# A two-dimensional Fourier mixing layer and a maxout network on one core: the sequence transform regrouped, with its intermediate sent through DRAM

## The chip, the core and the metric

The kernel runs on one core of one Trainium2 chip. The metric is the device time in microseconds of one execution. A core has five engines that run their own instruction streams in order: TensorE (PE, with weight loads shown as PEld), VectorE (DVE), ScalarE (ACT), GpSimd (POOL) and SyncE (SP), beside 16 DMA engines. SP and POOL issue most DMAs here.

## The reference

```python
X = np.fft.fft(x, axis=1)          # x: (8, 3072, 256), float32
X = np.fft.fft(X, axis=2)
x = X.real.reshape(24576, 256)
h = np.maximum(np.maximum(x @ w1, x @ w2), x @ w3)   # each w: (256, 768)
out = h @ w_out                                      # w_out: (768, 256), float32 result
```

There are eight batches of 3072 tokens with 256 features.

## The kernel before

Everything is bf16 with float32 accumulation. The feature transform (256 points) is folded into the weights at the start (`product`, `prep_first`, `prep_second`: tables `gE`, `gO`, `gD`, `gw`). What is left per batch is the sequence transform (3072 points), and then the network. The real part of a transform of real data has a symmetry, so only the frequencies 0 to 1535 are transformed (`NHALF`), as an even part `tE` and an odd part `tO`, each 128 x 1536; a token and its mirror come from sums and differences of the two.

**The main loop.** For each batch b there are three blocks of 512 tokens, and in each block six units (one for each 128 columns of the hidden layer), 18 units a batch (`UNITS`). A unit issues four matmuls of 128x512 for the token itself (`unit_plus`, L415 and L416), the activation and maximum of them (`unit_out`: L429 on ACT, L430 on DVE), two more 128x512 matmuls for the mirrored token of the unit before (`unit_minus`, L423), and then ten steps of the second layer of the block before (`l2_some(10)`: matmuls L439, L455 and L463, the sum on DVE at L468, and the stores). A 128-token result leaves by two stores: the tokens themselves by SP (L483) and the mirrored tokens, which stand in falling order, by an indirect DMA of POOL (L473).

**The transform of the next batch** is cut into pieces that a hand-written plan (`at(batch, unit, fn)`) puts at the ends of units, behind `l2_some(10)`. 3072 is handled as 24 times 128:

- `load_chunk` loads a quarter of the next x in float32 by four SP DMAs (L100) of 24 partitions each, in runs of 64 values (256 bytes). `turn_chunk` casts and reorders it on POOL (L118, four casts a batch).
- `s0` to `s12` (L337): 64 small matmuls a batch, with a 96x128 piece of x as the stationary operand and the constant `m24blk` (96x96) moving; ACT casts each group of five out of PSUM into `ub` (L339).
- `fA0` to `fC1` (`fold`, L350 to L373): DVE adds and subtracts mirrored halves of `ub` into `zE` and `zO`.
- `kE0` to `kO2` and `end` (L387 to L406): the second stage, six groups of 128-wide matmuls with `zE` and `zO` as stationary operand against the tables `cos_t`, `sin_t`, `nsin_t`; ACT casts each group into `tE` or `tO` (L399).

For batches from the third on, the pieces start at unit 5 of the batch before and end at unit 17. Batch 0 does all of this ahead of the main loop, after the tables have been made and after a few warm-up matmuls (L565).

Of the kernel before, what the change touches and what calls it, by code (L numbers as in the profile page):

```python
# [19 lines left out]
def _reduce(nc, w, v, q, period, rnd, neg):  # L20

    shape = list(v.shape)
    for c in (rnd, neg):
        assert c.shape[0] == shape[0]
    wide = [shape[0], v.free_size()]
    nc.vector.scalar_tensor_tensor(out=q, in0=v, scalar=1.0 / period,
                                   in1=rnd.to_broadcast(wide), op0=ALU.mult, op1=ALU.add)
    nc.vector.scalar_tensor_tensor(out=q, in0=q, scalar=-ROUND,
                                   in1=neg.to_broadcast(wide), op0=ALU.add, op1=ALU.mult)
    nc.vector.tensor_tensor(out=w, in0=v, in1=q, op=ALU.add)  # L30


@with_exitstack
def kernel(
# [18 lines left out]

    DLS = ((20, 25), (25, 30), (30, 35), (35, 40), (40, 45),
           (15, 20), (45, 50), (10, 15), (50, 55),
           (5, 10), (55, 60), (60, 64), (0, 5))
# [7 lines left out]
    xs_pool = ctx.enter_context(tc.tile_pool(name="xs", bufs=4))  # L64
    x0_pool = ctx.enter_context(tc.tile_pool(name="x0", bufs=2))
    u_pool = ctx.enter_context(tc.tile_pool(name="ubuf", bufs=1))
    z_pool = ctx.enter_context(tc.tile_pool(name="zbuf", bufs=1))
    t_pool = ctx.enter_context(tc.tile_pool(name="tbuf", bufs=2))

    m24blk = consts.tile([96, 96], BF16, tag="m24blk")  # L70
# [4 lines left out]
    cos_t = consts.tile([128, 13 * 128], BF16, tag="cos_t")  # L75
    sin_t = consts.tile([128, 13 * 128], BF16, tag="sin_t")
    nsin_t = consts.tile([128, 13 * 128], BF16, tag="nsin_t")
# [14 lines left out]
    zO = consts.tile([128, 26 * 128], BF16, tag="zO")  # L92

    def x_rows(b):
        return x[b].rearrange("(a bb) (g dl) -> g a bb dl", bb=128, g=4)

    def load_rows(eng, dst, b, r0, r1, after=None):
        xr = x_rows(b)
        for g in range(4):
            ld = eng.dma_start(out=dst[g * 24:(g + 1) * 24], in_=xr[g, :, r0:r1, :])  # L100
            if after is not None:
                tc.add_manual_dep(ld.ins, after.ins.name, AFTER, reason="weights first")

    def load_chunk(b, ch, after=None):
        xs = xs_pool.tile([96, 32 * 64], FP32, name="xs", tag="xs")
        load_rows(nc.sync, xs.rearrange("p (bb dl) -> p bb dl", dl=64), b,
                  ch * 32, ch * 32 + 32, after)
        return xs

    raw = {}  # L110
    turned = {}

    def turn_chunk(b, ch, after=None):

        if ch == 0:
            x0 = x0_pool.tile([96, 64 * 128], BF16, name="x0", tag="x0")
            turned[b] = x0.rearrange("p (dl bb) -> p dl bb", bb=128)
        cast = nc.gpsimd.tensor_copy(turned[b][:, :, ch * 32:(ch + 1) * 32],  # L118
                                     raw.pop((b, ch)).rearrange("p (bb dl) -> p dl bb", dl=64))
        if after is not None:  # L120
            tc.add_manual_dep(cast.ins, after.ins.name, AFTER, reason="folds first")
# [10 lines left out]
    HEAD = 80  # L132
    staged = []
    for (r0, eng) in ((80, nc.sync), (96, nc.scalar), (112, nc.sync)):
        xs = xs_pool.tile([96, 32 * 64], FP32, name="xs", tag="xs")
        load_rows(eng, xs[:, 0:16 * 64].rearrange("p (bb dl) -> p bb dl", dl=64), 0, r0, r0 + 16)
        staged.append((r0, xs))
# [3 lines left out]
    jm24 = gen.tile([96, 24], FP32, tag="jm24")  # L141
    iota(jm24[:, 0:13], [[1, 13]])
    iota(jm24[:, 13:24], [[-1, 11]], base=-1)
    g24 = gen.tile([96, 5], FP32, tag="g24")
    iota(g24, [[24, 5]])
    i13 = gen.tile([128, 13], FP32, tag="i13")
    iota(i13, [[1, 13]])
    j128 = gen.tile([128, 128], FP32, tag="j128")
    iota(j128, [[24, 128]])
    dvec = gen.tile([128, 128], FP32, tag="dvec")  # L150
    iota(dvec[:, 0:120], [[5, 12], [64, 2], [1, 5]])
    iota(dvec[:, 120:128], [[64, 2], [1, 4]], base=60)

    x0_first = x0_pool.tile([96, 128 * 64], BF16, name="x0", tag="x0")
    x0v = x0_first.rearrange("p (bb dl) -> p bb dl", dl=64)
    for (r0, r1) in ((0, 32), (32, 64), (64, 80)):
        load_rows(nc.gpsimd, x0v[:, r0:r1, :], 0, r0, r1)

    first_half = None
    for jh in range(2):  # L160
        for wsrc, wdst in ((moe_w1, w1_bf), (moe_w2, w2_bf), (moe_w3, w3_bf)):
            wld = nc.gpsimd.dma_start(
                out=wdst.rearrange("p (fc j) -> p fc j", fc=2)[:, :, jh * 384:(jh + 1) * 384],
                in_=wsrc.rearrange("(fc p) j -> p fc j", fc=2)[:, :, jh * 384:(jh + 1) * 384])
            if jh == 0 and wdst is w2_bf:
                first_half = wld
    nc.gpsimd.dma_start(out=wout_bf.rearrange("p (jc c) -> p jc c", jc=NJC),
                        in_=moe_w_out.rearrange("(jc p) c -> p jc c", jc=NJC))
    rows_f = gen.tile([128, 12 * B], FP32, tag="rows_f")
    rows_v = rows_f.rearrange("p (b r) -> p b r", r=12)  # L170
    iota(rows_v, [[S, B], [-1, 12]], base=S - 1, cm=-24)
    iota(rows_v[:, :, 11], [[S, B]], base=S - 24, cm=-24)
    late = gen.tile([128, 1], FP32, tag="late")
    nc.gpsimd.tensor_scalar(out=late, in0=pidx, scalar1=63.0, scalar2=float(S // 2 - 12),
                            op0=ALU.is_ge, op1=ALU.mult)
    nc.gpsimd.tensor_scalar(out=rows_v[:, :, 11], in0=rows_v[:, :, 11], scalar1=late,
                            scalar2=None, op0=ALU.add)
    nc.gpsimd.tensor_copy(rows_m, rows_f)
    zOr = zO.rearrange("p (r c) -> p r c", c=128)
    nc.gpsimd.memset(zO[:, 24 * 128:26 * 128], 0.0)  # L180
    nc.gpsimd.memset(zOr[:, 0:24, 0], 0.0)

    consts_of = {}
    for (name, value) in (("half_pi", 0.5 * math.pi), ("rnd", ROUND), ("n24", -24.0),
                          ("n256", -256.0), ("n3072", -3072.0)):
        c = gen.tile([128, 1], FP32, name=name, tag=name)
        nc.vector.memset(c, value)
        consts_of[name] = c
    s24 = gen.tile([96, 24], FP32, tag="s24")
    nc.vector.memset(s24[:, 0:13], 6.0)  # L190
    nc.vector.memset(s24[:, 13:24], 0.0)
# [4 lines left out]
    v24 = gen.tile([96, 24], FP32, tag="v24")  # L196
    q24 = gen.tile([96, 24], FP32, tag="q24")
    nc.vector.scalar_tensor_tensor(out=v24, in0=jm24, scalar=pidx[0:96], in1=s24,
                                   op0=ALU.mult, op1=ALU.add)
    _reduce(nc, v24, v24, q24, 24.0, consts_of["rnd"][0:96], consts_of["n24"][0:96])  # L200
    t24 = gen.tile([96, 24], FP32, tag="t24")
    nc.scalar.activation(out=t24, in_=v24, func=AX.Sin, scale=float(2.0 * math.pi / 24.0))
    ge24 = gen.tile([96, 5], FP32, tag="ge24")
    nc.vector.tensor_scalar(out=ge24, in0=g24, scalar1=pidx[0:96], scalar2=None,
                            op0=ALU.is_le)
    ind24 = gen.tile([96, 4], FP32, tag="ind24")
    nc.vector.tensor_tensor(out=ind24, in0=ge24[:, 0:4], in1=ge24[:, 1:5], op=ALU.subtract)
    pi13 = gen.tile([128, 13], FP32, tag="pi13")
    nc.vector.tensor_scalar(out=pi13, in0=i13, scalar1=pidx, scalar2=None, op0=ALU.mult)
    nc.vector.tensor_tensor(  # L210
        out=m24blk.rearrange("p (r g) -> p g r", g=4),
        in0=t24.unsqueeze(1).to_broadcast([96, 4, 24]),
        in1=ind24.unsqueeze(2).to_broadcast([96, 4, 24]), op=ALU.mult)

    w = gen.tile([128, 13 * 128], FP32, tag="w")
    v = gen.tile([128, 13 * 128], FP32, tag="v")
    q = gen.tile([128, 13 * 128], FP32, tag="q")
    turn = float(2.0 * math.pi / 3072.0)
    for (r0, r1) in ((0, 7), (7, 13)):
        cs = slice(r0 * 128, r1 * 128)  # L220
        n = r1 - r0
        nc.vector.scalar_tensor_tensor(
            out=v[:, cs].rearrange("p (r j) -> p r j", j=128),
            in0=j128.unsqueeze(1).to_broadcast([128, n, 128]), scalar=pidx,
            in1=pi13[:, r0:r1].unsqueeze(2).to_broadcast([128, n, 128]),
            op0=ALU.mult, op1=ALU.add)
        _reduce(nc, w[:, cs], v[:, cs], q[:, cs], 3072.0, consts_of["rnd"], consts_of["n3072"])
        nc.scalar.activation(out=sin_t[:, cs], in_=w[:, cs], func=AX.Sin, scale=turn)
# [503 lines left out]
```

## Time and profile before

| what | value |
|---|---|
| median of 3 runs | 432.07 us (430.92 to 433.14) |
| profiled execution: span from first to last instruction | 431.8 us |
| mean granted TensorE clock | 0.996 |
| busy: PE, DVE, ACT, POOL | 94%, 71%, 63%, 55% of the span |
| first unit of the main loop | starts at 33.2 us |
| DMA moved | 51.58 MB in 127333 packets, 109233 of them under 512 bytes |

The runs' times stand 0.3 us above the profiled span. The busy share of PE is a modelled one: matmuls overlap, so the pace of a group is read from the starts of its instructions, not from their durations.

### The profile page before, as it was taken

How to read it: one execution, taken by the hardware profiler on the slowest of the kernel's cores; microseconds unless marked ns; L12 is line 12 of the kernel's file. 1: busy time of each engine (PE TensorE's matmuls, PEld its weight loads, DVE VectorE, ACT ScalarE, POOL GpSimd, SP SyncE). 2: the span in 40 equal slices, each digit the busy share in tenths (PEclk: the TensorE clock that was granted, in tenths of full speed). 3: DMA queues.
4: the chain of work that ended last, by engine and by line, in shares of the span. 5: the costliest groups of instructions: out<-in, count | busy, mean ns of one | idle time of the engine just before them, and what ended most of it. 6: DMA issues, size and time to landing. Idle time of an engine off the chain costs nothing.

```text
span 431.8 us, 9121 instructions
## 1 busy us (share of the span) xinstructions
PE 404.8 (94%) x3196; PEld 271.1 (63%) x3252; DVE 307.7 (71%) x611; ACT 272.8 (63%) x512; POOL 238.0 (55%) x256
## 2 busy tenths in 40 slices
PE   0499979999999999999999999999999999999996
PEld 0175656666666666666666666667666666666665
DVE  7766748856886769576876679576876679667673
ACT  3576557666866676657765676757765676754650
POOL 7546762598249823984279624984369623214320
PEclk9989999999999999999999999999999999999999
DMA  9999999559731969159761969158762222111213
GB/s 115 111 160 124 128 139 192 152 113 174 147 107 53 179 131 204 63 99 160 145 145 73 167 127 199 73 97 155 148 141 74 74 63 74 62 56 52 105 66 130
DMA packets 127333, 51.58 MB, mean 119 GB/s; under 512 B 109233, under 2 KB 124344, under 8 KB 127288
## 3 DMA queue, kind: packets, MB, share of 16 engines
q1 hardware_dynamic: 104936, 35.80, 44.8%
q0 software_dynamic: 20624, 14.68, 17.8%
q10 hardware_dynamic: 1728, 0.52, 0.8%
q8 instruction: 25, 0.41, 0.4%
q14 instruction: 20, 0.16, 0.2%
HBM read 28.31 MB, written 25.17 MB: 124 GB/s over the span
## 4 chain that ended last, share of the span: by engine, by line
PE 84%; DVE 5%; ACT 4%; issue 2%; DMA 2%; POOL 1%; SPq 1%; ACTq 0%; DVEq 0%; POOLq 0%
PE po L439 27%; PE pse L415 14%; PE pse L423 13%; PE pse L416 11%; PE ps L337 6%; PE po L463 4%; PE pl L455 2%; DMA xs<-in_x_dram 2%; DVE hm L430 1%; ACT stmp L429 1%; PE warm L565 1%; PE psg L268 1%; PE ps L394 1%; DVE ot L468 1%; POOL x L118 1%
## 5 line engine op out<-in xcount | busy, mean ns | idle before, releaser
L429 ACT ACTIVATE stmp<-pse 128x512 bf16<-128x512 f32 x288 | 167.6, 605 | 57.4 <-PE pse L416 45.5
L473 POOL DMA_INDIRECT out_dram<-ot,rows_m x92 | 101.8, 1107 | 160.5 <-DVE ot L468 144.0
L430 DVE TENSOR_TENSOR hp<-pse,stmp 128x512 bf16<-128x512 f32 x144 | 99.3, 689 | 98.9 <-ACT stmp L429 64.9
L118 POOL CAST x<-xs 96x2048 bf16<-96x2048 f32 x28 | 104.6, 3745 | 11.3 <-DMA xs<-in_x_dram 8.8
L415 PE MATMUL pse<-tE,gE 128*128 128x512 bf16 x280 | 106.1, 379 | 2.2
L430 DVE TENSOR_TENSOR hm<-pse,stmp 128x512 bf16<-128x512 f32 x144 | 98.6, 685 | 6.3 <-ACT stmp L429 6.0
L416 PE MATMUL pse<-tO,gO 128*128 128x512 bf16 x245 | 92.7, 379 | 0.5
L439 PE MATMUL po<-wout_bf,hp 128*128 128x256 bf16 x576 | 86.1, 273 | 0.1
L423 PE MATMUL pse<-tO,gD 128*128 128x512 bf16 x284 | 84.9, 379 | 0.6
L439 PE MATMUL po<-wout_bf,hm 128*128 128x256 bf16 x576 | 78.6, 273 | 0.0
L339 ACT CAST ub<-ps 128x480 bf16<-128x480 f32 (+1 forms) x102 | 51.7, 556 | 37.2 <-PE ps L337 37.2
L439 PEld LDWEIGHTS <-hp 128*128 128x128 bf16 x576 | 56.4, 98 | 26.1
L439 PEld LDWEIGHTS <-hm 128*128 128x128 bf16 x576 | 56.4, 98 | 16.3
L468 DVE TENSOR_TENSOR ot<-po,even 128x512 f32<-128x512 f32 x92 | 62.7, 682 | 0.0
L423 PEld LDWEIGHTS <-gD 128*128 128x128 bf16 x288 | 27.7, 98 | 32.5 <-POOL gD L281 0.5
L416 PEld LDWEIGHTS <-gO 128*128 128x128 bf16 x288 | 28.1, 98 | 19.8 <-issue 1.6
L415 PEld LDWEIGHTS <-gE 128*128 128x128 bf16 x288 | 28.0, 97 | 19.5 <-issue 0.8
L337 PE MATMUL ps<-m24blk,x 96*128 96x96 bf16 x512 | 33.3, 213 | 2.7 <-POOL x L118 1.7
L463 PE MATMUL po<-gw,tO 128*128 128x512 bf16 x91 | 34.5, 379 | 0.0
L337 PEld LDWEIGHTS <-x 96*128 96x128 bf16 x512 | 30.5, 111 | 5.0 <-POOL x L118 2.0
L399 ACT CAST tO<-ps 128x512 bf16<-128x512 f32 x24 | 14.1, 586 | 22.4 <-PE ps L396 14.0
L459 ACT COPY even<-pl 128x512 f32<-128x512 f32 x46 | 27.3, 593 | 0.1
(127 smaller groups left out, 309.1 us busy)
## 6 DMA issues: line engine op xcount, KB each, us to landing
xs<-in_x_dram SPq DMA_DIRECT2D x112, 192.0 KB
out_dram<-ot SPq DMA_DIRECT2D x90, 128.0 KB
out_dram<-ot,rows_m POOLq DMA_INDIRECT x92, 4.4
w_bf<-in_moe_w_dram POOLq DMA_DIRECT2D x6, 192.0 KB, 5.6
out_dram<-ot SPq DMA_DIRECT2D x17, 64.0 KB
xs<-in_x_dram SPq DMA_DIRECT2D x8, 96.0 KB
x<-in_x_dram POOLq DMA_DIRECT2D x8, 96.0 KB, 11.5
xs<-in_x_dram ACTq DMA_DIRECT2D x4, 96.0 KB
```

What stands on the lines that cost most here:

```text
L118: cast = nc.gpsimd.tensor_copy(turned[b][:, :, ch * 32:(ch + 1) * 32], raw.pop((b, ch)).rearrange("p (bb dl) -> p dl bb", dl=64))
L337: nc.tensor.matmul(ps1[:, i * 96:(i + 1) * 96], x0[:, d0 + i, :], m24blk, start=True, stop=True)
L339: evict(out=self.ub[:, d0 * 96:d1 * 96].rearrange("p (c i) -> p c i", i=n), in_=ps1[:, 0:n * 96].rearrange("p (i c) -> p c i", c=96))
L415: nc.tensor.matmul(pse[:, 0:n], gE[i][:, js], te, start=True, stop=False)
L416: nc.tensor.matmul(pse[:, 0:n], gO[i][:, js], to, start=False, stop=True)
L423: nc.tensor.matmul(pse, gD[i][:, js], to, start=False, stop=True, skip_group_check=True)
L429: nc.scalar.activation(out=stmp[:, 0:n], in_=pses[0][:, 0:n], func=AX.Relu)
L430: nc.vector.tensor_tensor(out=dst, in0=src3, in1=stmp[:, 0:n], op=ALU.max)
L439: nc.tensor.matmul(po, hcols(jc), wout_bf[:, jc * 256:(jc + 1) * 256], start=False, stop=(jc == NJC - 1), skip_group_check=True)
L463: nc.tensor.matmul(po, to[:, cp], gw[:, 256:768], start=True, stop=True)
L468: nc.vector.tensor_tensor(out=ot.rearrange("p (h c) -> p h c", h=2), in0=po.rearrange("p (h c) -> p h c", h=2), in1=lin.unsqueeze(1).to_br ...
L473: stored(nc.gpsimd.indirect_dma_start(out, bass.IndirectOffsetOnAxis(ap=rows_m[0:128 - lo, b * 12 + slot: b * 12 + slot + 1], axis=0), ot[ ...
```

## The change

The sequence transform is regrouped as 96 runs of 32 rows each. A row index is `32 rows x 96` instead of `24 x 128`, and the folding of mirrored rows and mirrored features takes place inside the contraction of the first matmul.

- **x.** `load_x` brings each batch in by eight POOL DMAs of 32 partitions, in runs of 128 values (512 bytes), cast to bf16 on the way; half of them with the row order reversed. The feature half that has to be mirrored lands in `xm`, and DVE reverses it into `xt` (`mirror`, four pieces a batch, and `mirror_first`). The casts on POOL are gone. Batch 0 is loaded in float32 by 16 SP DMAs and cast by ACT and DVE.
- **First stage.** `s0` to `s5` are two matmuls each with a constant table (128x128) as stationary operand and 512 columns of x moving, `s6` is one of 128 columns. ACT casts the results into `tb`.
- **DRAM detour.** `y` writes `tb` to a DRAM tile (three SP DMAs a batch, of 64 partitions), and `z` reads it back into `yb` in another order (six SP DMAs, four of 24 partitions in runs of 256 bytes and two of one partition). The folds on DVE are gone.
- **x0.** Two small matmuls and an ACT copy fill one column of `yb`.
- **Second stage.** `k` has 19 matmuls of at most 96 columns for each of E and O, and `end` has two.
- **Stores.** The slots of 128 tokens now consist of two or three runs of rows 32 apart (`_runs`), so SP issues two or three stores for each slot.
- **Start.** Other tables with other index arithmetic; warm-up matmuls in three groups; batch 0 goes through the detour in two halves; the second half of the weights, `w_out` and x of batch 1 are loaded by POOL after the last `z` of batch 0 has landed.

```diff
-    def load_rows(eng, dst, b, r0, r1, after=None):
-        xr = x_rows(b)
-        for g in range(4):
-            ld = eng.dma_start(out=dst[g * 24:(g + 1) * 24], in_=xr[g, :, r0:r1, :])
...
-        cast = nc.gpsimd.tensor_copy(turned[b][:, :, ch * 32:(ch + 1) * 32],
-                                     raw.pop((b, ch)).rearrange("p (bb dl) -> p dl bb", dl=64))
...
+    def load_x(b, s0, s1, eng, dsts, after=None):
+        rows = x[b].rearrange("(a s) (m f) -> m a s f", s=96, m=2)
+        for m, dst in enumerate(dsts):
...
+            for h in range(2):
+                lo, hi = (s0, s1) if h == 0 else (max(s0, 1), min(s1, 48))
+                src = rows[m]
+                src = src[:, lo:hi, :] if h == 0 else src[:, 97 - hi:97 - lo, :][:, ::-1, :]
+                p0 = 64 * m + 32 * h
+                ld = eng.dma_start(out=dst[p0:p0 + 32, lo:hi, :], in_=src)
...
+    def mirror(b, s0, s1, src, fn):
+        fn(out=xt[b % 2][64:128, s0:s1, 1:128], in_=src[64:128, s0:s1, 127:0:-1])
...
-            for i in range(n):
-                nc.tensor.matmul(ps1[:, i * 96:(i + 1) * 96], x0[:, d0 + i, :], m24blk,
-                                 start=True, stop=True)
...
+            if k < 6:
+                for hh in range(2):
+                    nc.tensor.matmul(ps1, tab_at[hh], self.x[:, 8 * k + hh:8 * k + 8:2, :],
+                                     start=(hh == 0), stop=(hh == 1))
+                evict(out=tb[:, k * 512:(k + 1) * 512], in_=ps1)
...
+        def y(self, a=0, z=24, tail=True):
...
+            for hh in range(2):
+                d0 = hh * 24
+                nc.sync.dma_start(out=self.db[:, (d0 + a) * 128:(d0 + z) * 128],
+                                  in_=tb[hh * 64:hh * 64 + 64, a * 128:z * 128])
+            if tail:
+                nc.sync.dma_start(out=self.db[:, 48 * 128:49 * 128], in_=tbv[0:64, 24, :])
+
+        def z(self, spans=((0, 24),), tail=True):
+            for cs in range(2):
+                q0, n = cs * 2 * RI, 2 * RI - 4 * cs
+                src = self.db[q0:q0 + n].rearrange("q (s f) -> s q f", f=128)
+                dst = yb[:, 0:n * 128].rearrange("p (q f) -> p q f", f=128)
+                for (a, z) in spans:
+                    for hh in range(2):
+                        p0, p1 = cs * 64 + 2 * a + hh, cs * 64 + 2 * z
+                        last = nc.sync.dma_start(out=dst[p0:p1:2],
+                                                 in_=src[hh * 24 + a:hh * 24 + z])
...
+        def x0(self, evict=nc.scalar.copy):
...
+            for cs in range(2):
+                nc.tensor.matmul(psx[cs * 64:cs * 64 + 64, 0:RI], self.x[:, :, 0],
+                                 tabx[:, cs * RI:(cs + 1) * RI], start=True, stop=True)
+            evict(out=ybv[:, :, 1, 0], in_=psx[:, 0:RI])
...
+            special = {0: [(0, 0, 32)], 1: [(0, 0, 16), (16, 16, 16)], 2: [(16, 0, 32)]}[g]
+            parts = special + [(5 * g + 1 + i, 32 + 96 * i, 96) for i in range(5)]
...
+            for (r, c0, wd) in parts:
+                nc.tensor.matmul(ps2[:, c0:c0 + wd], ybv[:, (r - 1) % RI, which, :],
+                                 tab[:, g * 512 + c0:g * 512 + c0 + wd], start=True, stop=True)
...
+    load_w(1, y_first)
+    wld = nc.gpsimd.dma_start(out=wout_bf.rearrange("p (jc c) -> p jc c", jc=NJC),
...
+    for (s0, s1) in HALVES:
+        load_x(1, s0, s1, nc.gpsimd, (xt[1], xm))
...
-    begin = [9, 6] + [5] * (B - 3)
...
+    for ch in range(4):
+        at(0, (5, 6, 7, 8)[ch], lambda ch=ch: turn(1, ch))
+        at(0, (9, 11, 13, 15)[ch], lambda ch=ch: fetch(2, ch))
+        at(1, (0, 1, 2, 3)[ch], lambda ch=ch: turn(2, ch))
+    for b in range(3, B):
+        for ch in range(4):
+            at(b - 2, (4, 6, 8, 10)[ch], lambda b=b, ch=ch: fetch(b, ch))
+            at(b - 2, (13, 14, 15, 16)[ch], lambda b=b, ch=ch: turn(b, ch))
+
+    ahead0 = {9: ("s0", "s1"), 10: ("s2", "s3"), 11: ("s4", "s5"), 12: ("s6", "y"), 13: ("z",),
+              15: ("x", "kE0", "kO0"), 16: ("kE1", "kO1"), 17: ("kE2", "kO2", "end")}
+    ahead = {5: ("s0", "s1"), 6: ("s2", "s3"), 7: ("s4", "s5"), 8: ("s6", "y"), 9: ("z",),
+             11: ("x",), 12: ("kE0",), 13: ("kO0",), 14: ("kE1",), 15: ("kO1",),
+             16: ("kE2",), 17: ("kO2", "end")}
```

## The prediction

> **What bounds the kernel now.** First the page: which engine is full, and when.
>
> ```profile
> PE 404.8 (94%) x3196; PEld 271.1 (63%) x3252; DVE 307.7 (71%) x611; ACT 272.8 (63%) x512; POOL 238.0 (55%) x256
> ...
> PE   0499979999999999999999999999999999999996
> ```
>
> PE is full from the fourth slice on. As its busy time is modelled, the stretches of the main loop and PE's waits come next (first number: length, second: PE busy; at the end clock, DMA share, GB/s).
>
> ```profile
> 75.00:118.00 43.00, 42.60 (x353) 28.81 (x359) 31.24 (x64) 29.62 (x58) 27.05 (x24) 1.00 0.72 147
> 330.00:375.00 45.00, 44.68 (x358) 30.12 (x363) 33.21 (x67) 30.34 (x57) 19.27 (x26) 1.00 0.20 66
> PE ps L337 <- POOL x L118: 1.7, 1, 1.7
> PE ps L394 <- DVE zO L370: 0.6, 1, 0.6
> ```
>
> PE lacks 0.3 us in 45, and its only real stall after the start is one of 1.7 us (near 58 us, on the first cast x). So PE's own work sets the time: whatever leaves PE comes off the end, and any wait put into PE's stream goes on it. The timeline of PE gives the paces (start, length, group).
>
> ```profile
> 207.70 0.59 PE L337 MATMUL ps<-m24blk,x 96*128 96x96 bf16 x10
> 208.13 0.38 PE L415 MATMUL pse<-tE,gE 128*128 128x512 bf16 x1
> 208.35 0.38 PE L416 MATMUL pse<-tO,gO 128*128 128x512 bf16 x1
> ...
> 218.27 0.22 PE L387 MATMUL ps<-cos_t,zE 128*128 128x128 bf16 x1
> 218.33 0.22 PE L390 MATMUL ps<-sin_t,zE 128*128 128x128 bf16 x1
> ...
> 33.20 0.38 PE L415 MATMUL pse<-tE,gE 128*128 128x512 bf16 x1
> ```
>
> From start to start: ten 96-wide matmuls take 0.43 us (43 ns each), a 512-wide one 216 ns, a 128-wide one 56 ns. The main loop begins at 33.2 us. A unit without extra pieces takes 2.38 us (411.15 to 413.54 in the timeline). Last the DMA views.
>
> ```profile
> 38.00:56.00 18.00, 17.30 (x129) 10.84 (x131) 12.57 (x19) 11.15 (x21) 13.48 (x5) 1.00 1.04 130
> q1 hardware_dynamic: 9176, 2.31, 103.3%
> 236.58 10.11 SPq L100 DMA_DIRECT2D xs<-in_x_dram  x8
> DMA to landing us min/median/max: 2.4/4.4/11.5
> ```
>
> Line two is SP's queue in the stretch of line one: 9176 packets in 18 us, 510 a microsecond, with runs of 256 bytes into 24 partitions, the form that `z` will have. Line three: eight such loads (6144 runs) issue in 10.1 us, 608 a microsecond. Line four is the landing of the 128 KB scatter.
>
> **PE's work, per batch.** Out: 64 x 43 ns = 2.75; second stage 44 x 56 ns, six 64-wide at 30 ns and three tiny at 25 ns = 2.7. In: first stage 12 x 216 ns + 0.06 = 2.65; `x0` 0.06; second stage 30 96-wide and 8 narrow; `end` 0.05. The 96-wide ones now have full 128-row weights, so 43 ns (same width) to 56 ns (same weights); I take 43, since width set the pace in both rows: 1.3 + 0.2 = 1.5. Sum 5.45 - 4.25 = 1.2 us less (0.8 at the other end). Seven batches give 8.4; of batch 0 only four second-stage groups lie in the loop, 0.7. **PE: -9.1.** The 128-row moving operand in the first stage makes it no cheaper: 2.75 against 2.65.
>
> **The 1.7 us stall and the 0.4 us wait near it: -2.2.** x of batch 1 should land by 50 us (below) and is first wanted by DVE at unit 5 of batch 0, about 55 us.
>
> **Off PE.** ACT loses 13 casts of 0.56 and gains seven; DVE loses folds (54 us over the run, 6.8 a batch) and gains four mirrors of some 1524 elements. Their price lies between 0.95 us (fold of 720 elements in 0.52, two elements a nanosecond) and 1.9 us (512 in 0.69); nearest is the float32 cast of 1024 in 0.68, a one-source SBUF copy, so 1.0. POOL loses 28 casts of 3.75 and gains 56 load issues of 0.84. SP issues some 13 more stores a batch at 0.38. All of it hides under PE while no engine is at 100% over a unit; DVE comes nearest in units 13 to 16: 1.83 + 1.0 against PE's 2.38 + 0.27. I take 0.
>
> **The detour.** In the steady plan `s6` and `y` stand at the end of unit 8, `z` at 9, `x0` at 11, `kE0` at 12. Count from T, the end of unit 8. PE wants `kE0` at T + 9.6 (four units). But ACT's copy of `x0` writes into `yb`, so it too waits for `z`, at T + 7.2, and behind it in ACT's queue stand the activations of units 11 and 12, which free the PSUM that PE needs in unit 13; ACT has about 1 us of slack a unit. So `z` must have landed by about T + 8.5 to 9.
>
> `y`: three issues of 0.4 and 0.79 MB. At the highest rates of the before (about 340 GB/s over a microsecond) 2.3 us, and a landing of about 2 (scatter: 2.4, of which 0.4 is data). Two of the three can go about 1 us ahead of T, their pieces being ready: landed at T + 3.5 to 4.5. `z` waits for that. It is 3136 runs of 256 bytes: 6.2 us at 510 a microsecond, 5.2 at 608, and 1.5 to 2 to land. Alone the round trip ends between T + 10 and T + 12.5. It is not alone: loads of x two batches on are issued at units 4, 6, 8 and 10, 1600 runs each. Bounds for what they add: 0 (they fall between) and the whole of two loads, about 6 us. Nearest row, 8 to 13 us, where POOL's casting queue and SP's ran together:
>
> ```profile
> q0 software_dynamic: 3334, 0.31, 192.6%
> q1 hardware_dynamic: 1127, 0.28, 56.9%
> ```
>
> SP's queue got 225 a microsecond there instead of 510. An overlap of about 3 us then adds some 1.5 to 2. I take `z` at T + 13, a PE stall of 4 us, in the five batches transformed beside such loads (2 to 6); 2.5 in batch 7, which has none; 5.5 in batch 1, whose plan leaves three units instead of four. **Detour: +28** (0 to +52).
>
> In the Trainium skill, DMA: Bandwidth & Descriptors, section Queues, rings and completion order, each DMA engine serves its queues in turn, a packet at a time. By that rule `z` would run at half pace whenever x runs; the 225 of 510 agrees. That is the rival "shared engines" below.
>
> Behind SP's wait for `y` stand the stores of units 9 to 12; six output buffers cover nine units, so 0 (if that cover went, DVE would wait at its sum).
>
> **The start.** Before, the second stage begins at 30.85 and the loop at 33.2. Now ACT makes the feature tables (about 12 us: a longer chain of small DVE steps at 0.2 each, and the table load behind them), then casts x (2048 elements, 2.1 each by the 0.95 for 896), 1.8 of tables, two more casts, and only then the PSUM of `s1`: about 21. First `y` lands at 24.5, its `z` is issued, then the second `y` behind it on SP lands at 30, the second `z` at 35. Only then does POOL load the second half of the weights (three issues of 0.72, landing 4.1 to 6.8 in the before), which the first `prep_some` needs ahead of unit 0: 39.5, then x of batch 1 by about 50. **Start: +6.3** (+3 to +10).
>
> **Sum.** Against the profiled span of 431.8: -9.1 - 2.2 + 6.3 + 28 = 454.8, and the runs' median stood 0.3 above the span: 455. If the loads cost nothing and the round trip fits, it is 427.
>
> **Rivals.** *The round trip fits* (26%). `z` issues at 608 a microsecond or more, `y` goes early, x falls between, and `z` lands by T + 9: the stalls vanish, 427 (422 to 431), faster. For: the fastest stretch of the before; against: it needs every bound at its best, and batch 1 has a unit less.
>
> *Shared engines, cold clock* (13%). x and `z` overlap fully: 8 us of stall in batches 2 to 6, 2.5 in batch 7, 9.5 in batch 1, 52 in all, 479. In the before the mean clock between 21.6 and 33.2 us was 0.85, where PE paused for half a microsecond at a time: a loss of 0.15 x 11.6 = 1.7 us. If each of six such stalls brings that loss again, 10 more, 489. The Trainium skill, TensorE: Matmul & The Clock Gate, Part 1, says that an idle window of about 3.4 us halves the clock; by it stalls under 3.4 us cost nothing more.
>
> *DVE becomes the bound* (7%). The round trip fits, but mirrors cost 1.9: DVE then needs 3.7 us in each of units 13 to 16 against PE's 2.65, 4.2 a batch less 1 of slack, over six batches 20: 447. It decides from a mirror of about 1.1 us.
>
> **Chances.** The forecast (stalls of 2 to 6 us a batch; 443 to 466) has 54%. Half a percent, 2.2 us, is about what a measurement can tell from no change: 429.9 to 434.2 counts as the same. Of the first rival 22% lies below that and 4% in it; with 1% of the forecast's lower edge: faster 0.22, same 0.05, slower 0.73. The range is 424 to 478: it leaves out the quicker start with no stall (about 7%) and most of the second rival (about 11%).
>
> **What would show it.** Right: PE idle ahead of `kE0` in each batch, ended by a DMA into `yb`, ACT waiting for the same DMA at the copy of `x0`; SP waiting for `db`; first unit near 39.5; 96-wide matmuls 43 ns apart. Wrong: PE full through units 9 to 13, `yb` landing before unit 11 ends; or PE waiting for DVE in units 13 to 16; or a first unit before 36 us.

## The result and the profile after

The changed kernel takes 542.55 us (median of 4 runs, 541.56 to 544.03) against 431.59 for the kernel before beside it: a ratio of 1.256, 95% interval 1.250 to 1.261. The profiled span grew from 431.8 to 539.8 us, by 108. The page of the kernel after answers the page of before: engine sums, the busy tenths of PE, its clock, and the chain that ended last.

```profile
PE 416.9 (77%) x2716; PEld 255.8 (47%) x2764; DVE 299.2 (55%) x503; ACT 255.6 (47%) x470; POOL 180.6 (33%) x276
PE   0646996499719995599919997399926999499996
PEclk9966999599958998699968999699986999699999
PE 63%; DMA 15%; SPq 11%; DVE 3%; ACT 3%; issue 3%; POOL 1%; ACTq 0%; DVEq 0%
```

PE has 480 matmuls fewer, and seven dips behind the start, one for each batch after the first; the clock falls in the same slices. A quarter of the chain now lies in DMAs and in SP's issuing of them. The waits of the kernel after (total in us, times, longest) say on what:

```profile
PE ps L401 <- ACT yb L392: 64.2, 5, 14.4
PE ps L401 <- DMA yb<-db: 16.3, 4, 5.7
PE psg L292 <- DMA w_bf<-in_moe_w_dram: 7.4, 2, 4.5
ACT yb L392 <- DMA yb<-db: 81.7, 6, 17.6
ACT yb L392 <- DMA out_dram<-ot: 24.6, 2, 14.9
```

L401 is the second stage (`kE0`), L392 ACT's copy of `x0`, which shares `yb` with `z`. Two of ACT's waits, and PE's 6.5 us in batch 7, bear the name of a store (`out_dram`). That is no sign that a store holds them up: stores and `z` on SP's queue use the same semaphores in turn, and in batch 3, where ACT's wait of 14.9 us bears a store's name, the last two semaphore events of `z`'s own reads come at 221.29 and 221.48 us in the trace and ACT starts at 221.57. Ahead of `kE0` PE stands still for 5.7 + 5.5, 14.4, 11.8, 11.8, 12.2, 13.9 and 6.5 us in batches 1 to 7: 81.9 us. In batch 3 the timeline of SP's queue shows the round trip (start, length, line; L365 and L368 are `y`, L378 the 24-partition and L382 the one-partition reads of `z`, L482 stores):

```profile
198.49 1.10 SPq L365 DMA_DIRECT2D db<-tb  x2
200.50 0.45 SPq L368 DMA_DIRECT2D db<-tb  x1
203.24 2.00 SPq L482 DMA_DIRECT2D out_dram<-ot  x2
205.35 1.79 SPq L378 DMA_DIRECT2D yb<-db  x2
207.24 3.39 SPq L382 DMA_DIRECT2D yb<-db  x1
210.68 3.93 SPq L378 DMA_DIRECT2D yb<-db  x2
214.65 3.29 SPq L382 DMA_DIRECT2D yb<-db  x1
```

T, the end of `s6` on PE, is 200.0. `z` begins to issue at T + 5.4, behind the stores at 203.24; it takes 12.6 us to issue six DMAs, and PE goes on at 221.86, T + 21.9 (T + 22 to 24 in batches 4 to 6). PE's own work had ended at T + 10.1. The DMA view of 205 to 218 us shows what ran meanwhile (packets, MB, share of 16 engines):

```profile
q0 software_dynamic: 3419, 1.25, 73.7%
q1 hardware_dynamic: 3255, 0.91, 34.7%
```

q1 is SP's queue with `z`: 250 packets a microsecond, where the prediction had 510 to 608. q0 is POOL's queue with casting loads of x, issued at 200.57 and 206.91 (after units 8 and 10).

**Where 108 us went.** The stalls are 81.9. The start is 15.1: the first unit begins at 45.03 instead of 33.20, and `kE1` of batch 0 at 53.95 instead of 38.88. The last unit's end to the end of the span is 1.1 longer. The rest of the loop gains 6.6 of PE (0.94 a batch, from spread below) and the 2.1 of the old waits. That makes 89.4; the missing 18.6 is 2.65 for each of seven stalls. It lies in the units behind a stall: batch 3 to 4, `kE0` to `kE0`, takes 61.82, which is 47.45 (an undisturbed batch in spread) + 11.84 of stall + 2.53.

### The profile page after: what moved, and what is told of

The parts are those of the page before. It is cut to its first block, busy times and chain, and to the rows that moved or that the text cites. A ratio compares the mean times of both kernels' runs of the same rounds, so it can differ in the third digit from the quotient of the medians.

```text
span 539.8 us, 8153 instructions
## 1 busy us (share of the span) xinstructions
PE 416.9 (77%) x2716; PEld 255.8 (47%) x2764; DVE 299.2 (55%) x503; ACT 255.6 (47%) x470; POOL 180.6 (33%) x276
## 4 chain that ended last, share of the span: by engine, by line
PE 63%; DMA 15%; SPq 11%; DVE 3%; ACT 3%; issue 3%; POOL 1%; ACTq 0%; DVEq 0%
PE po L442 21%; PE pse L418 11%; PE pse L426 11%; PE pse L419 10%; DMA yb<-db 7%; SPq L378 7%; DMA db<-tb 6%; SPq L382 4%; PE ps L352 3%; PE po L465 3%; PE ps L401 2%; PE pl L457 1%; DVE hm L433 1%; DMA wout_bf<-in_moe_w_out_dram 1%; ACT stmp L432 1%
## 5 line engine op out<-in xcount | busy, mean ns | idle before, releaser
L475 POOL DMA_INDIRECT out_dram<-ot,rows_m x92 | 107.3, 1166 | 323.0 <-DVE ot L470 304.2
L432 ACT ACTIVATE stmp<-pse 128x512 bf16<-128x512 f32 x288 | 169.6, 600 | 85.8 <-PE pse L419 53.8
L418 PE MATMUL pse<-tE,gE 128*128 128x512 bf16 x280 | 109.3, 390 | 4.7 <-ACT stmp L432 1.7
L419 PE MATMUL pse<-tO,gO 128*128 128x512 bf16 x258 | 100.5, 390 | 0.8 <-issue 0.4
L426 PE MATMUL pse<-tO,gD 128*128 128x512 bf16 x283 | 87.7, 391 | 0.4
L442 PE MATMUL po<-wout_bf,hm 128*128 128x256 bf16 x576 | 82.0, 280 | 0.0
L401 PE MATMUL ps<-te_tab,yb 128*128 128x96 bf16 (+2 forms) x152 | 12.1, 216 | 87.0 <-ACT yb L392 64.2
L401 PEld LDWEIGHTS <-yb 128*128 128x128 bf16 x304 | 18.2, 103 | 89.9 <-issue 81.9
L392 ACT CAST yb<-psx 128x17 bf16<-128x17 f32 x8 | 1.9, 234 | 106.3 <-DMA yb<-db 81.7
L354 ACT CAST tb<-ps 128x512 bf16<-128x512 f32 x45 | 24.2, 588 | 24.8 <-PE ps L352 24.8
L352 PE MATMUL ps<-xt,tabz 128*128 128x512 bf16 x96 | 25.5, 389 | 2.7 <-DVE xt L129 2.7
```

The costliest lines, as they stand in the source:

```text
L352: nc.tensor.matmul(ps1, tab_at[hh], self.x[:, 8 * k + hh:8 * k + 8:2, :], start=(hh == 0), stop=(hh == 1))
L401: nc.tensor.matmul(ps2[:, c0:c0 + wd], ybv[:, (r - 1) % RI, which, :], tab[:, g * 512 + c0:g * 512 + c0 + wd], start=True, stop=True)
L418: nc.tensor.matmul(pse[:, 0:n], gE[i][:, js], te, start=True, stop=False)
L419: nc.tensor.matmul(pse[:, 0:n], gO[i][:, js], to, start=False, stop=True)
L426: nc.tensor.matmul(pse, gD[i][:, js], to, start=False, stop=True, skip_group_check=True)
L432: nc.scalar.activation(out=stmp[:, 0:n], in_=pses[0][:, 0:n], func=AX.Relu)
```

## Experiments

The theory after the result: `z` takes 22 us from T, because x's loads run beside it, and its deadline is T + 10; all else follows. (The runs below bear out about half of it: the round trip is too long for its deadline even without x.) Rivals: the time lies in fixed costs of the round trip; in the one-partition DMAs; or in the slow clock behind each stall. All times stand against 539.8 of span or 542.55 of run time.

**early** gives the round trip of batches 3 to 7 five more units, that of batch 2 two more.

```diff
-    ahead = {5: ("s0", "s1"), 6: ("s2", "s3"), 7: ("s4", "s5"), 8: ("s6", "y"), 9: ("z",),
...
+    ahead = {0: ("s0", "s1"), 1: ("s2", "s3"), 2: ("s4", "s5"), 3: ("s6", "y"), 4: ("z",), **late}
```

> Only the plan moves: the first stage, y and z of batches 3 to 7 stand at units 0 to 4 of the batch before instead of 5 to 9, those of batch 2 at units 3 to 7; the second stage stays at units 11 to 17, and tE and tO are allocated at the first second-stage group instead of at the first-stage one. Batch 1 stays as it is. Theory A (PE loses its time because z lands about 21 us after the end of s6, where the plan leaves 7 to 10): the pauses ahead of kE0 vanish for batches 3 to 7 (56.3 us together in the changed kernel), that of batch 2 falls from 14.4 to about 9.5, that of batch 1 stays near 11; with the half clock behind each pause about 470 us. Rival (the DMA engines are simply full, or x0's copy or the stores behind z are what stops PE): the pauses stay or move to other units, and the time stays within 15 us of 542.

Measured 503.26. The stalls shrank, to 7.0, 5.7, 3.0 and 6.5 in batches 3 to 6 (and none in 7), but stayed. With `s6` at 186.9 in batch 3, five units earlier in the plan, `kE0` started at 216.0: now T + 29. `z` now ran beside all four loads of x instead of two. A longer time for `z` was filled by x.

**x_later** takes x away from `z` and leaves `z` where it was.

```diff
-            at(b - 2, (4, 6, 8, 10)[ch], lambda b=b, ch=ch: fetch(b, ch))
-            at(b - 2, (13, 14, 15, 16)[ch], lambda b=b, ch=ch: turn(b, ch))
+            at(b - 2, (13, 14, 15, 16)[ch], lambda b=b, ch=ch: fetch(b, ch))
+            at(b - 1, (0, 1, 2, 3)[ch], lambda b=b, ch=ch: turn(b, ch))
```

> The x loads for batches 3 to 7 are issued by POOL at units 13 to 16 instead of 4, 6, 8 and 10, and mirrored in the next batch's units 0 to 3: no load of x runs beside y and z of batches 2 to 6. Theory A1 (x on POOL's queue halves z's pace): those five pauses fall from 11.8 to 14.4 to the 6.5 that batch 7 has without such loads, some 32 us and the half clock less, about 500 us. Rival A2 (z's own form is slow): the pauses stay above 10, about 540 us.

Measured 516.32; the stalls of batches 3 to 7 are 5.3, 6.4, 6.7, 7.3, 6.6, where batch 7 of the changed kernel, without x, had 6.5. So the stalls fell as the theory had it; the time, put at about 500, did not fall as far. The DMA view of 202 to 210 us, the same `z` as above:

```profile
q1 hardware_dynamic: 3259, 0.86, 47.5%
q0 software_dynamic: 137, 0.38, 14.1%
```

3259 packets in 8 us instead of 3255 in 13. In batch 3 `z` issues from T + 5.0 for 7.9 us and PE goes on at T + 15.4; in batches 4 to 7 at T + 16.5 to 17.4. So x costs 6.5 us of the 21.9 in batch 3 and 5.4 to 6.7 in batches 4 to 6, and 15.4 to 17.4 us remain without x. What it is in these loads that slows `z`, their cast, their short runs or their amount, was not separated.

**no_tail** and **x_later_no_tail** leave out the DMAs of `y` and `z` with one partition (`yb` then lacks the last pair of rows), with x beside `z` and without.

```diff
-            if tail:
-                nc.sync.dma_start(out=self.db[:, 48 * 128:49 * 128], in_=tbv[0:64, 24, :])
...
-                    last = nc.sync.dma_start(
-                        out=dst[p0:p0 + 1],
-                        in_=src[48:49])
```

> The one-partition DMAs of y and z (the 49th run of rows) are left out, so one row in 49 of the first-stage result does not reach the second stage; all else is the same. Theory A2 (the two one-partition reads, issued in 3.3 us each, run on few engines and hold up SP's queue): each pause is 4 to 6 us shorter, about 500 us. Rival A1 (x on the other queue): SP's queue is slow for the large reads anyhow, and the pauses shrink by under 1.5 us, about 535 us.

> As x_later, with the DMAs of y and z that go to or from a single partition left out (so the last pair of rows is missing in yb). Theory (in x_later the round trip takes 14.6 us, of which the two one-partition reads, whose 34 and 30 packets follow each other at about 0.17 us, hold the queue for some 3 to 4 us when x is not beside them): the stalls of batches 3 to 7 fall from 6.5 to 3 to 4 us, the time to about 500. Rival (they are hidden behind the other four as they were with x beside them, where leaving them out gained 0.6 us a batch): stalls 5.5 to 6.5, time 512 to 516.

Measured 537.6, 5 less than the changed kernel, and 514.97, 1.3 less than x_later. The stalls of x_later_no_tail in batches 3 to 7 are 6.2, 6.0, 5.6, 7.1 and 5.9. The 3.3 us that L382 takes in SP's timeline are time in which the queue waits for what lies ahead: without it the other reads take longer to issue (one takes 4.5 us in no_tail's batch 3, one 3.4 in that of x_later_no_tail). The one-partition DMAs are no more than a small part of the 108 us.

**long_runs** keeps bytes, partitions and DMAs of `z`, but each partition reads one piece instead of 30 or 34 runs of 256 bytes (`yb` then does not hold the regrouped values).

```diff
-                        last = nc.sync.dma_start(out=dst[p0:p1:2],
-                                                 in_=src[hh * 24 + a:hh * 24 + z])
+                        ins, outs = src[hh * 24 + a:hh * 24 + z], dst[p0:p1:2]
+                        if z - a == 24:
+                            ins, outs = self.db[q0:q0 + 24, 0:n * 128], yb[p0:p1:2, 0:n * 128]
+                        last = nc.sync.dma_start(out=outs, in_=ins)
```

> In the main loop z reads the same number of bytes into the same partitions by the same six DMAs, but each partition's bytes lie in one piece (8.7 or 7.7 KB) instead of 34 or 30 runs of 256 bytes; so yb does not hold the regrouped values. Theory (what makes z late is the number of runs, 3136 a batch, and their slow pace beside x): z issues in 1 to 3 us and lands 2 to 3 us later, about 8 us after the end of the first stage, inside the 9.6 that it has; the stalls of 12 us fall to 0 to 3 and the time to 450 to 470. Rival (the time is in fixed costs of the round trip, waits for y, queue order and landing, or in the bytes beside x): the stalls keep at least 8 us each, time above 505.

Measured 509.95, between the two. SP's timeline in batch 3, where T is 188.3 (L381 and L384 are `z`):

```profile
194.03 1.56 SPq L381 DMA_DIRECT2D yb<-db  x2
195.80 0.62 SPq L384 DMA_DIRECT2D yb<-db  x1
196.46 1.47 SPq L381 DMA_DIRECT2D yb<-db  x2
197.97 0.81 SPq L384 DMA_DIRECT2D yb<-db  x1
```

Even with 24 pieces a DMA, six issues take 4.8 us, and `kE0` starts at T + 17.7. In batch 7, without x, PE goes on at T + 14.9 (434.86), against T + 16.7 with short runs, in the changed kernel and in x_later alike. So the number of runs costs 4.2 us beside x in batch 3 (up to 6.2 in batch 6) and 1.8 alone. The 14.9 depend neither on x nor on the number of runs: 5.4 us until SP has come past two stores and issues `z`, 5.2 for six issues, 4.3 for landing. So both the theory and its rival of fixed costs are right in part: of the 11.8 us by which `z` is late in batch 3, x makes 6.5, and 5.3 are there without it.

**kept_busy** fills the stalls with matmuls whose results are not used, so that the clock stays up.

```diff
+        if what == "x":
+            keep = ps_f.tile([128, 512], FP32, name="keep", tag="ps")
+            for _ in range({1: 50, 7: 28}.get(b, 54)):
+                nc.tensor.matmul(keep, md_all[:, 0:128], md_all, start=True, stop=True)
```

> Ahead of x0 of each batch in the loop PE issues idle-filling 512-wide matmuls into an unused PSUM tile: 54 (11.7 us), 50 for batch 1, 28 for batch 7. They replace the wait by work, so z lands at the same time. Theory B (behind each pause PE runs 3.4 to 6 us at half clock, and ACT and DVE have to restart): the clock stays at 1.0 in the loop, and the time falls by 14 to 20 us, to 522 to 528. Rival (the pause alone costs, the clock nothing): 540 or above.

Measured 537.49, only 5 less. The window of 222 to 231 us, behind batch 3's stall, first in kept_busy and then in the changed kernel (busy time and count of PE, PEld, DVE, ACT, POOL; then the clock):

```profile
222.00:231.00 9.00, 8.03 (x68) 5.36 (x67) 7.18 (x12) 6.42 (x13) 1.25 (x2) 1.00 0.10 31
```

```profile
222.00:231.00 9.00, 8.47 (x55) 4.99 (x56) 5.83 (x9) 5.65 (x11) 1.25 (x2) 0.77 0.10 31
```

At full clock PE does 68 matmuls instead of 55 in 9 us, and is 1.3 us ahead five units later (the next batch's first unit starts at 236.6 instead of 238.1, from 221.63 and 221.86). But `kE0` to `kE0` it gains only 0.1 (61.73 against 61.82): T of batch 4 comes 1.3 us sooner after batch 3's `kE0`, but `z` then begins to issue at T + 6.8 instead of T + 5.1 and PE goes on at T + 23.1 instead of T + 21.9. Why that round trip was longer was not traced. Half of the 2.5 us behind a stall is the clock. In the other half PE waits for ACT and DVE (0.46 us each behind this stall of kept_busy), whose work stood behind ACT's copy of `x0`.

**placed** changes the plan, so that all is early enough (the stages as in early, those of batches 1 and 2 moved likewise) and x out of the way, and loads the weights' second half early; **early_w** does the last part alone (the first two edits).

```diff
     load_w(0, second_chunk)
+    load_w(1)
...
-    load_w(1, y_first)
...
-            at(b - 2, (4, 6, 8, 10)[ch], lambda b=b, ch=ch: fetch(b, ch))
-            at(b - 2, (13, 14, 15, 16)[ch], lambda b=b, ch=ch: turn(b, ch))
+            at(b - 2, (10, 11, 12, 13)[ch], lambda b=b, ch=ch: fetch(b, ch))
+            at(b - 2, (14, 15, 16, 17)[ch], lambda b=b, ch=ch: turn(b, ch))
```

> Only the plan is changed: first stage, y and z of each batch move to the first units of the batch before (units 0 to 4; batch 1: 5 to 9 of batch 0, batch 2: 1 to 5 of batch 1), the loads of x to units 10 to 13, their mirrors to units 14 to 17 (and mirror_first goes with each piece), and the second half of the weights is loaded right behind the first. Theory (the stalls are a matter of when things are issued: z needs 15 us from the end of the first stage when alone, and now has 20): all seven stalls ahead of kE0 vanish, the first unit starts near 40 instead of 45, and the time is that of before (431.8) less 9.1 of PE and 2.2 of stall, plus 6.8 of start and 1.2 of tail: 428, range 425 to 436. Rival (the detour loads the DMA engines or SP so much that something else becomes late, such as stores, mirrors on DVE or x): stalls of 2 to 4 us a batch stay in other places, 440 to 460.

> The second half of the weights is loaded right behind the first, ahead of the detour of batch 0, instead of behind its last z; all else as in the changed kernel. Theory (the late first unit is one chain: last z, then the issue of the weights, then their landing): the stall of 4.5 us ahead of the second half's first product goes, the first unit starts near 40 instead of 45, and the time falls by 4 to 5 to about 535. Rival (the weights share the DMA engines with the detour's z of batch 0, whose runs then slow down): z of batch 0 lands 3 to 5 us later and the first unit stays at 44 to 45, time 539 to 541.

placed: 468.1 to 471.2, ratio 1.089 (1.084 to 1.093). In batches 3 to 7 no stall ahead of `kE0` is left, but one of 1.9 to 2.6 us appeared in unit 16 of four batches, and DVE's timeline says why:

```profile
204.05 0.62 DVE L125 COPY xt<-xm_t 64x1651 bf16<-64x1651 bf16 x1 [3.73 <-DMA xm_t<-in_x_dram]
```

The mirror stood in DVE's queue before x had landed, and the maxima behind it waited. early_w: 542.07, nothing gained. The weights then share the DMA engines with batch 0's round trip, whose `kE0` moves from 36.0 to 39.8 us. The rival was right.

**products_later** makes the first product of the weights' second half at the end of unit 1 instead of ahead of unit 0; **rows_first** also makes the index table `rows_f` on POOL ahead of the loads.

```diff
-    load_w(1, y_first)
...
     dve(out=rows_m, in_=rows_f)
+    load_w(1, y_first)
...
     m.k(0, 0)
     m.k(1, 0)
-    prep_some()
...
-    for (u, fn) in ((0, prep_some), (0, prep_some), (1, prep_some),
+    for (u, fn) in ((1, prep_some), (1, prep_some), (1, prep_some),
```

The first two edits are rows_first's own.

> Only the start of the changed kernel is altered: the first product of the weights' second half is made at the end of unit 1 instead of ahead of unit 0. Theory (the first unit waits for the weights, not for the transform): unit 0 starts near 39.5 to 40 instead of 45.0 and the time falls by 4 to 5 to about 536. Rival (what is gained ahead of unit 0 is waited for again at units 1 to 3, where the second half is needed, or in batch 1, whose x comes at the same time as before): time within 2 us of the changed kernel's 540 to 542.

> As products_later, and also the index table rows_f is made on POOL ahead of the loads of weights and x, so that DVE's last step of it (which stands ahead of the first unit's maximum) does not wait for POOL to issue them. Theory (DVE's wait for rows_f at 49.2 us is what held units 1 and 2): the stall of 7.7 us at unit 1 goes, and about 7 of it comes off the end: 534 to 536. Rival (the products of the weights' second half are then waited for at unit 1, or batch 1's x is): time above 539.

products_later: first unit at 39.6, and 542.3 in all, nothing gained: PE stops for 7.7 us in unit 1. DVE's timeline of that run:

```profile
49.30 0.26 DVE L614 TENSOR_TENSOR rows_f<-rows_f,adj 128x96 f32<-128x96 f32 x1 [15.76 <-POOL rows_f L137]
```

The table is made on POOL, behind twelve load issues that themselves wait for the last `z`; DVE needs it ahead of its first maximum. rows_first: 535.03, 7.3 less; no stall in unit 1.

**placed_again**, **one_order** and **spread** are three more plans with the late products (the last two with the early table too), in which x keeps away from `z`. The diff is that of spread, with u = 3, 2, 1, 0, 0, 0 for batches 2 to 7; in one_order batches 2 to 7 have their first stage in units 4 to 7, and batch 1 in units 5 to 8.

```diff
-            at(b - 2, (4, 6, 8, 10)[ch], lambda b=b, ch=ch: fetch(b, ch))
+            at(b - 2, {2: 14, 3: 13, 4: 12, 5: 11}.get(b, 9) + ch, lambda b=b, ch=ch: fetch(b, ch))
...
+    def ahead(u, rest):
+        return {u: ("s0", "s1"), u + 1: ("s2", "s3"), u + 2: ("s4", "s5"), u + 3: ("s6", "y"),
+                u + 4: ("z",), **rest}
```

> A second placing of the same work: as in placed, but the weights wait for the last z of batch 0 again, the products of their second half are made from unit 1 on instead of ahead of unit 0, the loads of x for batches 1 and 2 and the stages of batches 1 to 3 are spread so that no x is loaded beside a z, and of each x the half that must be mirrored is loaded first. Theory (the detour costs nothing where z has about 15 us and no x beside it; the rest of the loss in placed was the first batch and a 2 us wait for mirrors in each batch): first unit near 40, no stall above 1 us in batches 2 to 7, a batch in 47.3 us (placed without its wait) against 48.9 before, sum 40 + 48.5 + 6 x 47.3 + 56 = 428, range 424 to 436. Rival (z needs more than its own time, whatever is beside it, because stores share SP's queue with it): stalls of 2 to 4 us ahead of kE0 remain, 440 to 455.

> One order for all batches in which no x is loaded beside a z: loads of x at units 15 to 17 and 0, mirrors at units 2 to 5, first stage at units 4 to 7, y at 7, z at 8, x0 at 13, the second stage in units 14 to 17; at the start the index table rows_f is made ahead of the weights' and x loads on POOL, and the first product of the second half of the weights comes after unit 1. Theory (z is starved by x, and otherwise lands 15 us after the first stage): no stall ahead of kE0 above 2 us in any batch, first unit at 39.5 and no wait at unit 1, time placed_again's 464.7 less its stalls of 12.7, its 8.2 at unit 1 and some 5 of restarts: 436 to 440. Rival (the 15 us hold only with the extra units, and in units 8 to 13 the stores on SP's queue slow z again): stalls of 2 to 4 us a batch, 450 to 465.

> As one_order at the start and in batch 0, but the transform then moves forward by one or two units a batch (first stage from unit 3, 2, 1 and then 0 of the batch before), each z in the six units after it free of x, so that kE0 comes eight or nine units (19 to 22 us) after the end of the first stage in every batch instead of seven. Theory (the round trip takes up to 19 us even without x, and nothing else is lost in the loop): no stall ahead of kE0 above 1 us, batches of 47.4 us as in batches 3 to 6 of placed_again; 39.7 + 53.3 + 6 x 47.4 + 56.8 = 434, range 431 to 440; what is left against 431 is the start. Rival (z lands as late as it may, since stores on the same queue go ahead of it or beside it): stalls of 1 to 3 us a batch, 442 to 455.

placed_again: 464.72, ratio 1.078 (1.076 to 1.081). Batches 4 to 7 run without a stall at 47.45 us from `kE0` to `kE0`, against 48.39 before; what is lost lies in the start and in batches 2 and 3, where x and `z` still met. The DMA view of 141 to 147 us there, in batch 2, is the plainest row on the sharing:

```profile
q0 software_dynamic: 2978, 0.76, 136.4%
q1 hardware_dynamic: 1068, 0.28, 23.4%
```

x moves 496 packets a microsecond, `z` 178 (by the shares of 16 engines, a packet of x takes 44 ns and one of `z` 21). In batch 3 it was a tail: 3139 packets of 256 bytes on SP's queue lie between 182 and 191 us, ahead of x, and the last 61, most of them 0.05 or 0.17 us apart, between 191 and 197, beside 1860 of x. ACT's copy waits for them until 197.53. Whether x or something else made this tail so slow is not shown.

one_order: 458.57, ratio 1.063 (1.059 to 1.067). No x is beside any `z`, and `kE0` comes seven units after `s6`, but stalls of 1.2 to 2.55 us remain, two of them in batch 2: the rival was right that 15 us is not always enough. Where it stalls, `kE0` goes on 18.5 to 22.5 us after T. About 3 to 4 us of that is `y`, which here is issued at T + 1.4 to 2.5; in the changed kernel it was 1.5 us ahead of T.

spread: 436.71 against 432.15, ratio 1.014 (1.010 to 1.018), as expected. The first line of its page, and the window of two whole batches:

```profile
PE 401.5 (92%) x2716; PEld 250.4 (58%) x2764; DVE 299.9 (69%) x524; ACT 256.4 (59%) x470; POOL 179.9 (41%) x276
```

```profile
238.00:333.00 95.00, 94.37 (x653) 59.84 (x663) 68.16 (x114) 60.98 (x115) 41.95 (x64) 1.00 0.79 135
```

After the first unit no stall of a microsecond is left. The plan alone, with the start's two moves, takes back 106 of 111 us. The first unit still begins at 39.7 instead of 33.2.

**spread_start** tries to win that back: half of batch 0's last `z` goes to ACT's queue, and warm-up matmuls fill PE's pause.

```diff
+    y_first = m.z(((12, 24),), css=(1,), eng=nc.scalar)
...
     m.x0()
+    warm_up(14)
```

> As spread, but of the last z of batch 0 half is issued by ACT's queue, behind the tables, instead of all by SP, and 14 warm-up matmuls stand behind x0 of batch 0, so that PE does not pause for 2.7 us ahead of the second stage. Theory (in spread only the start is behind the kernel before: SP's issue of z from 31.8 to 36.8 us, and the half clock from 36.3 to 43.1 us): first unit at 37.5 to 38.5 at full clock, time 432 to 434, no difference to the kernel before that can be measured. Rival (the last z is bound by the landing and the packets, not by its issue; the warm-up goes beside other waits): first unit at 39.5 to 40.5, time 435.5 to 438.

Measured 441.31, ratio 1.023 (1.018 to 1.028): slower than spread. The first unit began at 38.5, as the theory said, and at full clock; but on ACT the casts of `gO` now stand behind two waits for `y`, POOL's `gD` and weights behind them, and unit 2 begins at 48.0 instead of 46.0. A stall of 1.5 us ahead of `kE0` of batch 4 came as well; the rest of the difference was not traced. No version beat the kernel before.

## Why the prediction was wrong

The sign and the mechanism were right: PE idle ahead of `kE0`, ACT held at the copy of `x0`, both ended by the DMA into `yb`. The time, 455 with an upper end of 478, missed by 88.

- **PE's work, -9.1: about right.** 47.45 against 48.39 us a batch: 0.94 less instead of 1.2, inside the bounds of 0.8 and 1.2; 96-wide matmuls follow each other in 42 ns (43 was taken).
- **Off PE, 0: right.** A mirror takes 0.56 to 0.62 us (1.0 was taken), so the rival "DVE becomes the bound" had no ground.
- **The deadline: right.** T + 8.5 to 9.6 was said; PE ran dry at T + 10.1.
- **The detour, +28: the step that failed.** The stalls took 81.9 us. `z` was put at T + 13 and PE went on at T + 21.9. Term by term in batch 3: `y` at T + 3.5 to 4.5, measured 5.4 until `z` issues, with two stores in between that the sum did not have; `z`'s issue 5.2 to 6.2, measured 7.9 alone and 12.6 beside x; landing 1.5 to 2, measured 2.5 alone and 3.9 beside x; x's overlap 1.5 to 2, measured 6.5 in all. The pace of 510 to 608 runs a microsecond came from long trains of x loads; `z` alone came to 407 as a mean (3259 packets in 8 us). And an overlap of 3 us with x was assumed where the two loads after units 8 and 10 run beside most of `z`.
- **What follows a stall: left out.** 2.5 us each, half of it clock, 18 in all. The second rival had priced the clock at 1.7 a stall; 1.3 was measured in batch 3, and taking it away bought 5 us in all, since the round trip behind it grew.
- **The start, +6.3: 15.1.** The 39.5 of the prediction had the product ahead of unit 0 in it; with it the weights, issued only at 38.4 behind `z`, landed at 43.8, and the first unit began at 45.03. That products_later, without that product, begins at 39.6 is chance. Another part, DVE waiting for a table that POOL makes behind those loads, was in no step; it was worth 7.3 us once the product was late.
- **The rival "shared engines, cold clock"** had the right cause, at 479 to 489 still too low: it took 8 us a stall, 52 in all.

By the Trainium skill, DMA: Bandwidth & Descriptors, Queues, rings and completion order, an engine serves its queues in turn, packet by packet, and a packet there holds several descriptors (about 9 to 17). The rows above show unequal counts: 178 packets of `z` a microsecond beside 496 of x in placed_again, 250 beside 263 in the changed kernel. But they count pieces of about 256 bytes, so they do not settle whether the turns were equal.

## What to carry to other kernels

A round trip through DRAM has a latency made of waits, issues and landings, which the bytes do not tell: here it took 15 to 17 us without x beside it. So place the whole trip first (here eight or nine units of 2.4 us), and keep other large loads out of its window: x cost it 5 to 7 us, and the weights in early_w held up batch 0's `kE0` by 3.8. Cost what stands in a queue behind a wait, too: the copy on ACT, the table on POOL and the mirror on DVE each held up work that did not need the data.

## What was not expected of the hardware

- Beside POOL's casting loads, whose packets take 44 ns in the row above, SP's reads fell to 178 packets a microsecond in one stretch and 250 in another, against 407 over a whole `z` without them (x_later).
- An issue of `z` on SP took 0.6 to 0.8 us when nothing held it up (long_runs, batch 3) and up to 3.7 us in the changed kernel. The long time can stand at a DMA that is not slow itself: with L382 left out it moved to other reads.
- A pause shorter than expected can halve the clock. In one_order PE paused for 2.35 us up to 338.05, and the clock of the next 4 us was 0.57:

```profile
338.05 0.37 PE L399 MATMUL ps<-te_tab,yb 128*128 128x96 bf16 x5 [2.35 <-DMA yb<-db]
```

```profile
338.00:342.00 4.00, 3.59 (x19) 1.69 (x20) 1.93 (x3) 3.02 (x7) 0.00 (x0) 0.57 0.27 75
```

The Trainium skill, TensorE: Matmul & The Clock Gate, Part 1, puts the idle window at about 3.4 us; here a shorter pause was enough. Length alone does not decide it below that: in placed, the clock of 4 us was 1.00 behind a pause of 2.55 us (206 to 210) and 0.57 behind one of 2.33 us (306 to 310). Pauses of 1.2 to 1.4 us in one_order left it at 1.
